# Narrow attention units in the last two batches, masks made on another engine, and a new order of work

## The chip, the cores and the metric

The kernel runs on one core of a Trainium2 chip. A core has TensorE (PE, matrix multiplies; its weight loads are listed as PEld), VectorE (DVE), ScalarE (ACT), GpSimd (POOL) and SyncE (SP). Each of them works through its own queue of instructions in order, and they wait for each other by semaphores. Data comes from the chip's memory by DMA; a DMA is started by an instruction in the queue of POOL or SP. The metric is device time in microseconds (us), lower is better.

## The reference

Two stages, for 8 batches of 576 tokens. The first is attention with 8 heads of 64 dimensions. A query sees itself and the 127 keys before it; a bias that grows linearly with the distance, with a slope for each head, is taken off the scores:

```python
scores = scale * q @ k.T            # scale = 1/8
rel    = pos[:, None] - pos[None, :]
mask   = (rel >= 0) & (rel < 128)
scores = where(mask, scores - slope[h] * abs(rel), -1e9)
attn   = softmax(scores) @ v        # slope[h] = 2 ** -(h + 1)
```

The second takes the heads side by side as x (576 x 512 for each batch) and mixes the tokens:

```python
W   = 1/8 * (x @ w_q) @ (x @ w_k).T     # 576 x 576
out = relu(W @ x) @ w_out
```

The kernel computes W @ x as (x @ w_q) times ((x @ w_k).T @ x), so that the 576 x 576 matrix is never made.

## The kernel before

**Stages of a batch.** For each batch b the kernel makes operations with names that are used below. `L` loads a block of q, k or v, with a conversion from 32 to 16 bit, by a DMA that POOL issues (`Lq`, `Lk`, `Lv` for blocks of 128 tokens, `Lt` for the last 64 tokens of q and k of two batches, and `Lv.4` for those of v). `TQ` and `TT` turn q and k on TensorE, by multiplying with an identity, so that the 64 dimensions of a head lie on the partitions; `ETQ` and `ETT` copy the result from PSUM into `qkT`. The q and k blocks 0 and 1 of batch 0 alone come by SP as 32 bit values and are converted on the chip (`C`).

`QK` computes scores, keys on the partitions and queries along the columns. A unit is 128 keys by 256 queries (the keys' own block and the next) for four of the eight heads; so `add_unit` is called for four groups g of keys and two halves u of the heads, eight units a batch. The last group has 192 + 64 columns, for keys 384 to 511 and the 64 keys after them. A unit fills two PSUM banks with 1024 columns. `EXP` on ACT takes the exponential of these into a tile `pt` (L680), and `MUL` on DVE multiplies with a table of exp(bias), zero where the mask forbids (L687). `PV` uses a piece of `pt` as weights and v with a column of ones as the moving side, so that column 64 of each head is the sum for the softmax; `X` on DVE takes the reciprocal and multiplies (L729, L730), and x is left in 16 bit.

Then `XT` turns x on TensorE, `WQ` and `WK` project it, `G` forms (x @ w_k).T @ x, `MX` multiplies, `RM` applies the relu, `OUT` multiplies with w_out, `EO` copies the result out of PSUM and `DO` sends it off. A name with E in front is the copy out of PSUM, on ACT or DVE.

**Constants.** POOL makes an identity in 32 bit (a memset and an affine select), which DVE converts to 16 bit; it writes the distances with iota, DVE converts them, and POOL sets what the mask forbids to 1e9 with two affine selects. ACT makes the tables `bias` with eight exponentials, one for each head, and DVE copies a second arrangement, `biasl`, for the last group. `zerop` zeroes the end of each `pt`, `ones` sets the column of ones in the v tiles.

**Tiles on TensorE.** Operations differ in how the 128 x 128 array is used, which the kernel calls a mode. Transposes, QK and MX use half the rows (64 x 128, written 64*128 in the profile), so two matmuls on the two halves run together. PV, WQ, WK and OUT use it whole. G uses half the columns (128*64). All matmuls and transposes are issued on L344 and L347.

**The order of work.** The order on each engine is fixed when the program is built. `Order.solve` is a list scheduler: of the operations that can start on an engine within `WINDOW` of the earliest, it takes the one with the lowest number in the table `WANT`, with assumed durations for each operation, four PSUM pairs, and a cost `SWITCH` for a change of mode on TensorE. Results of batches 1 to 5 (`LATE`) are sent from POOL and only after all loads have been issued; the others go by SP. Until 45 us of planned time (`WARM`) gaps on TensorE are filled with multiplies of zeros (`fill`).

Of the kernel before, what the change touches and what calls it, by code (L numbers as in the profile page):

```python
# [14 lines left out]
P = 128  # L15
S = 576
D = 64
# [10 lines left out]
NPT = 5  # L28
PTW = 1088

# [3 lines left out]
STRIDE = 15.2  # L34
BEGIN = {"PE": 0.6, "ACT": 2.0, "DVE": 1.15, "POOL": 1.25, "SP": 0.74, "Q": 0.0}
WARM = 45.0
LAG = 1.1
HELD = 23
# [6 lines left out]
    "ident": -41.18, "idh": 86.52, "iota": -19.88, "dist": -5.89, "zeros": 80.97, "zerop":  # L45
    -1.07, "mask": -22.91, "bias0": -63.72, "bias1": 51.34, "ones0": 9.03, "ones1": -3.39,
    "ones2": 1.11, "ones3": -22.77, "pads": 114.59, "biasl0": 1.04, "biasl1": 135.13, "Cq0.0":
    -16.2, "Ck0.0": -88.36, "Cq0.1": -9.63, "Ck0.1": 2.01, "Lq0.2": -29.16, "Lk0.2": -19.81,
    "Lq0.3": -23.26, "Lk0.3": -32.4, "Lv0.0": -19.56, "Lv0.1": -19.41, "Lt0.0": -19.68, "Lt0.1":
    -19.8, "Lv0.2": -18.96, "Lv0.3": -18.57, "Lv0.4": -18.52, "Lq1.0": -19.26, "Lk1.0": -19.37,  # L50
    "Lq1.1": -19.31, "Lv1.0": 22.81, "Lk1.1": -19.57, "Lw.0": 11.09, "Lw.1": -9.38, "wqq": 9.6,
    "Lq1.2": -17.78, "Lv1.1": 27.97, "Lk1.2": -16.76, "Lq1.3": -17.36, "Lv1.2": 25.83, "Lk1.3":
    -17.32, "Lv1.3": 28.25, "Lwo.0": 22.86, "Lwo.1": 22.17, "Lwo.2": 18.37, "Lwo.3": 22.81,
    "TQ0.0": 34.99, "ETQ0.0": -6.58, "TQ0.1": 52.99, "ETQ0.1": -272.3, "TQ0.2": -141.25,
    "ETQ0.2": -59.41, "TQ0.3": 42.12, "ETQ0.3": 0.07, "QK0.0.0": -12.02, "EXP0.0.0": 42.07,
    "MUL0.0.0": 21.76, "QK0.0.1": 130.94, "EXP0.0.1": -14.28, "MUL0.0.1": -21.15, "PV0.0":
    -15.02, "X0.0": -34.4, "QK0.1.0": -32.06, "EXP0.1.0": -89.58, "MUL0.1.0": -34.39, "QK0.1.1":
    -30.17, "EXP0.1.1": -84.62, "MUL0.1.1": -26.17, "PV0.1": -16.94, "X0.1": -55.8, "XT0.0":
    63.02, "EXT0.0": 6.73, "WQ0.0": -26.32, "EWQ0.0": 45.13, "TT0": -30.36, "ETT0": -52.54,
    "ETT1": -52.67, "QK0.2.0": -30.31, "EXP0.2.0": -89.02, "MUL0.2.0": -34.35, "QK0.2.1": 19.3,  # L60
    "EXP0.2.1": -69.71, "MUL0.2.1": -54.24, "PV0.2": 7.99, "X0.2": -64.32, "QK0.3.0": -21.53,
    "EXP0.3.0": -67.77, "MUL0.3.0": -42.2, "QK0.3.1": 13.11, "EXP0.3.1": -67.85, "MUL0.3.1":
    126.66, "PV0.3": -62.99, "X0.3": -65.12, "PV0.4": -86.99, "X0.4": -63.82, "XT0.1": 75.52,
    "EXT0.1": 12.55, "XT0.2": 53.95, "EXT0.2": -81.4, "WQ0.1": -51.64, "EWQ0.1": 61.61, "WK0":
    18.47, "EWK0": 19.41, "G0": 52.22, "EG0": -68.42, "MX0.0": -35.21, "RM0.0": -24.12, "RM0.2":
    -6.99, "MX0.1": 12.48, "RM0.1": -43.21, "RM0.3": -42.66, "MX0.2": -15.09, "RM0.4": -62.57,
    "OUT0.0": 3.34, "EO0.0": 15.12, "DO0.0": 34.49, "OUT0.1": 15.99, "EO0.1": 48.36, "DO0.1":
    34.7, "OUT0.2": 22.6, "EO0.2": 30.45, "DO0.2": 31.54, "OUT0.3": 22.73, "EO0.3": 55.07,
    "DO0.3": 27.61, "Lq2.0": 25.78, "Lk2.0": 29.91, "Lq2.1": 27.85, "Lv2.0": 36.01, "Lk2.1":
    24.01, "Lq2.2": 30.59, "Lv2.1": 34.45, "Lk2.2": 30.81, "Lq2.3": 31.03, "Lv2.2": 39.03,  # L70
# [117 lines left out]
class Op:  # L188


    def __init__(self, kind, b, part, want, on, deps, emit, banks=0, frees=None, mode=0, half=None):
        self.kind, self.batch, self.part = kind, b, part
        self.name = f"{kind}{b}" + (f".{part}" if part != "" else "")
        self.want, self.on, self.emit = want, on, emit
# [816 lines left out]
```

## Time and profile before

| | |
|---|---|
| median of 3 runs | 140.56 us (140.37 to 140.99) |
| profiled execution | 141.34 us, span 139.5 us |
| granted TensorE clock | 0.997 |
| PE busy | 129.3 us, 93% of the span, 2344 matmuls |
| PEld busy | 81.2 us, 58% |
| ACT busy | 115.2 us, 83% |
| DVE busy | 112.6 us, 81% |
| POOL busy | 110.0 us, 79% |

The span runs from the first to the last instruction of the program. Busy time of PE holds the filler too, 52 matmuls and 15.4 us, and ends of matmuls are modelled, so a busy PE may still be waiting. POOL's busy time is nearly all issue of DMAs.

### The profile page before, as it was taken

Reading aid. Unit: us, or ns where it says so; the run is one execution under the profiler, and the core shown is the slowest. Engines: PE = TensorE matmul, PEld = TensorE weight load, DVE = VectorE, ACT = ScalarE, POOL = GpSimd, SP = SyncE. Lnnn points to the kernel's source line nnn. Section 1 sums busy time; section 2 is a strip of 40 time slices with the busy share of each in tenths; the row PEclk is TensorE's granted clock in tenths of the full one; section 3 lists DMA queues with packets and bytes.
Section 4 is the critical chain, followed back from the end, with each engine's and each line's share of the span. In section 5 each row is a group of like instructions: output and inputs, shape, how many; then the busy total and the mean of one; then the engine's idle time right before and its main releaser. Section 6 shows DMA issues by size and latency. Waiting matters only on the chain.

```text
span 139.5 us, 5462 instructions
## 1 busy us (share of the span) xinstructions
PE 129.3 (93%) x2344; PEld 81.2 (58%) x2344; DVE 112.6 (81%) x250; ACT 115.2 (83%) x175; POOL 110.0 (79%) x145
## 2 busy tenths in 40 slices
PE   6999859998999999988999999999999999999980
PEld 2345447554676367766757567765666666865530
DVE  6648997659987899989999998899999989984400
ACT  6176988399669999999999989999999999676660
POOL 7899988899995899999999999999977745600000
PEclk9999999999999999999999999999999999999998
DMA  4999999999999999999999999999999993730494
GB/s 98 184 180 154 158 153 168 152 146 154 188 215 206 158 159 153 156 155 155 154 156 153 157 156 155 159 153 156 156 215 413 358 327 144 260 153 5 167 320 189
DMA packets 117127, 25.12 MB, mean 180 GB/s; under 512 B 113072, under 2 KB 114096, under 8 KB 117104
## 3 DMA queue, kind: packets, MB, share of 16 engines
q0 software_dynamic: 110912, 20.32, 169.0%
q1 hardware_dynamic: 6192, 4.46, 10.8%
q8 instruction: 18, 0.29, 0.8%
q14 instruction: 5, 0.04, 0.1%
HBM read 29.62 MB, written 9.44 MB: 280 GB/s over the span
## 4 chain that ended last, share of the span: by engine, by line
PE 60%; DVE 16%; POOL 8%; ACT 6%; DMA 5%; issue 2%; ACTq 0%; POOLq 0%; DVEq 0%
PE pair L344 52%; PE pair L347 8%; DVE pt L687 6%; DMA nat<-in_q_dram 5%; POOL nat L506 4%; ACT pt L680 4%; DVE x L730 3%; POOL vt L521 1%; POOL natt L513 1%; DVE inv L729 1%; DVE xtl L730 1%; DVE wqT L353 1%; DVE qkT L359 1%; DVE rm L843 1%; ACT xT L357 1%
## 5 line engine op out<-in xcount | busy, mean ns | idle before, releaser
L680 ACT ACTIVATE pt<-pair 128x1024 f16<-128x1024 f32 x64 | 62.2, 1034 | 2.3 <-PE pair L344 1.7
L687 DVE TENSOR_TENSOR pt<-pt,bias 128x1024 f16<-128x1024 f16 x48 | 32.0, 684 | 2.5 <-ACT pt L680 2.3
L344 PE MATMUL pair<-wout_sb,rm 128*128 128x512 f16 (+1 forms) x132 | 31.7, 373 | 0.2
L521 POOL DMA_DIRECT2D vt<-in_v_dram x32 | 30.1, 995 | 1.6 <-DMA natt<-in_q_dram 0.8
L506 POOL DMA_DIRECT2D nat<-in_k_dram x30 | 29.1, 997 | 0.5 <-DMA nat<-in_k_dram 0.3
L506 POOL DMA_DIRECT2D nat<-in_q_dram x30 | 29.0, 987 | 0.4 <-DMA natt<-in_k_dram 0.4
L344 PEld LDWEIGHTS <-pt 128*128 128x128 f16 x576 | 20.5, 97 | 6.2 <-issue 2.6
L344 PE MATMUL pair<-vt,pt 128*128 128x65 f16 x512 | 22.9, 193 | 0.4 <-ACT pt L680 0.4
L730 DVE TENSOR_TENSOR x<-pair,inv 128x512 f16<-128x512 f32 x32 | 22.1, 692 | 1.1
L344 PE MATMUL pair<-qkT 64*128 64x256 f16 (+2 forms) x320 | 22.1, 250 | 0.6 <-ACT pt L680 0.3
L351 ACT COPY osb<-pair 128x512 f32<-128x512 f32 x29 | 17.0, 596 | 5.7 <-PE pair L344 5.5
L344 PEld LDWEIGHTS <-rm 128*128 128x128 f16 x132 | 11.3, 97 | 11.8 <-issue 1.7
L357 ACT COPY qkT<-pair 128x1024 f32<-128x1024 f32 (+1 forms) x12 | 11.4, 949 | 7.7 <-PE pair L347 7.7
L344 PE MATMUL pair<-fill 128*128 128x512 f16 x52 | 15.4, 430 | 1.8 <-DVE fill L487 1.2
L918 POOL DMA_DIRECT2D out_dram<-osb x20 | 11.2, 574 | 6.6 <-ACT osb L351 3.6
L344 PEld LDWEIGHTS <-qkT 64*128 64x128 f16 x320 | 11.1, 94 | 8.0 <-issue 5.2
L347 PE MATMUL pair<-identh,nat 64*128 64x64 f16 x512 | 10.7, 190 | 1.3 <-DMA nat<-in_q_dram 0.9
L347 PEld LDWEIGHTS <-nat 64*128 64x128 f16 x512 | 9.2, 95 | 4.0 <-DMA nat<-in_q_dram 1.3
L687 DVE TENSOR_TENSOR pt<-pt,biasl 128x1024 f16<-128x1024 f16 x16 | 10.8, 683 | 0.0
L344 PE MATMUL pair<-xT,wqq_sb 128*128 128x320 f16 (+1 forms) x64 | 10.5, 286 | 0.3 <-DVE xT L359 0.3
L357 ACT COPY xT<-pair 128x512 f32<-128x512 f32 (+1 forms) x14 | 7.4, 527 | 3.6 <-PE pair L347 2.9
L359 DVE COPY qkT<-pair 128x512 f16<-128x512 f16 (+2 forms) x14 | 9.3, 686 | 1.3 <-PE pair L347 1.1
(63 smaller groups left out, 165.5 us busy)
## 6 DMA issues: line engine op xcount, KB each, us to landing
out_dram<-osb POOLq DMA_DIRECT2D x20, 256.0 KB, 4.6
vt<-in_v_dram POOLq DMA_DIRECT2D x32, 128.0 KB, 5.9
nat<-in_k_dram POOLq DMA_DIRECT2D x30, 128.0 KB, 6.0
nat<-in_q_dram POOLq DMA_DIRECT2D x30, 128.0 KB, 6.1
out_dram<-osb SPq DMA_DIRECT2D x11, 256.0 KB, 2.3
out_dram<-osb POOLq DMA_DIRECT2D x6, 128.0 KB, 4.2
natf<-in_q_dram SPq DMA_DIRECT2D x2, 256.0 KB, 4.7
natf<-in_k_dram SPq DMA_DIRECT2D x2, 256.0 KB, 5.4
```

The costliest lines, as they stand in the source:

```text
L344: hold(nc.tensor.matmul(*a, **k))
L347: hold(nc.tensor.transpose(*a))
L351: hold(nc.scalar.copy(out_ap, in_ap))
L353: hold(nc.vector.tensor_copy(out=out_ap, in_=in_ap))
L357: hold(nc.scalar.copy(out_ap.bitcast(FP32), in_ap.bitcast(FP32)))
L359: hold(nc.vector.tensor_copy(out=out_ap, in_=in_ap))
L506: return lambda: nc.gpsimd.dma_start(out=nat_s[b % NNAT][j][n], in_=src[b, :, P * n:P * n + P, :].transpose([1, 0, 2]))
L521: return lambda: nc.gpsimd.dma_start(out=vt_s[b % NV][t][:, :, 0:D], in_=v[b, :, P * t:P * t + P, :].transpose([1, 0, 2]))
L680: nc.scalar.activation(out=pt[:, 0:1024], in_=two(s.bank).rearrange("p e c -> p (e c)"), func=AF.Exp, scale=SCALE)
L687: ENG2[o.eng].tensor_tensor(out=pt[:, 0:1024], in0=pt[:, 0:1024], in1=bt, op=ALU.mult)
L730: nc.vector.tensor_tensor(out=x[r].rearrange("p (g h d) -> p g h d", g=2, h=4), in0=pxv[r, :, :, 0:64], in1=inv[r].unsqueeze(3).broadcast_ ...
L918: q.dma_start(out=out[b, P * st:P * st + P, c], in_=osb)
```

## The change

The change has these parts.

- **Narrow units** (`NARROW = (3,)`: the pair of batches 6 and 7). A unit is 64 keys by 192 queries for all eight heads: heads 0 to 3 have their keys on partitions 0 to 63, heads 4 to 7 on 64 to 127. `add_unit` is called as often as before, eight times a batch; unit 7 also holds the last 64 keys. The scores use quarters of the array (64 x 64), a unit has 768 columns, and so have its EXP and MUL. PV (`npv`) multiplies 64 keys at a time, on half of the rows, with two to four blocks of keys for each block of queries. v is loaded in four DMAs a batch, for two heads and all 576 keys each, 64 partitions of 18 rows. A narrow PV waits for all four. The other batches keep the old units (`add_wunit`, `wpv`).
- **Buffers.** `pt` is ten single tiles in place of five pairs. Narrow units use other columns of it, so before the first ten of them an operation `RZ` on DVE zeroes the columns between. The v tiles are used in two layouts, and `ones` is set again when a tile changes layout. QK now lists the release of its `pt` as a need, as EXP did.
- **Constants.** `make_identity` and the affine selects on POOL go. DVE compares the iota with zero for the identity, and makes the mask with multiplies and maxima, once for 256 columns and once for 192. ACT makes a second table of four exponentials for narrow units.
- **The planner.** Each TensorE operation has a count of its instructions. `solve` holds that TensorE's instructions come in blocks of `CHUNK` = 256, that it has `AHEAD` = 191 at first, and that a block comes no sooner than `FETCH` after the one before, and adds the wait.
- **The order.** `WANT` is another table, and `STRIDE`, for defaults, is 13.2 in place of 15.2.

```diff
-NPT = 5
+NPT = 10
 PTW = 1088
+W = 192
+NARROW = (3,)
...
-STRIDE = 15.2
+STRIDE = 13.2
...
+FETCH = 4.8
+CHUNK = 256
+AHEAD = 191
...
+            if eng == "PE" and op.count:
+                gap, wait = at - free["PE"], 0.0
+                if at < WARM and gap > 0.25:
+                    sent += 2 * int(gap / (0.43 if at < COLD else 0.216))
+                while sent > mark:
+                    came = max(at, came + (FETCH if came < 104.0 else FETCH - 1.0) if mark > AHEAD else 0.0)
+                    mark += CHUNK
+                    wait = max(wait, came - at)
+                if sent + op.count > mark:
+                    then = at + wait + occ * (mark - sent) / op.count
+                    least = came + (FETCH if came < 104.0 else FETCH - 1.0) if mark > AHEAD else 0.0
+                    wait += max(0.0, least - then)
+                    came = max(then, least)
+                    mark += CHUNK
+                sent += op.count
+                end, occ = end + wait, occ + wait
...
-    def mk_ident(o):
-        make_identity(nc, ident32)
-
...
-    def mk_mask(o):
-        nc.gpsimd.affine_select(out=wm, in_=wm, compare_op=ALU.is_ge, fill=1.0e9, base=0,
-                                pattern=[[1, 256]], channel_multiplier=-1)
-        nc.gpsimd.affine_select(out=wm, in_=wm, compare_op=ALU.is_ge, fill=1.0e9, base=127,
-                                pattern=[[-1, 256]], channel_multiplier=1)
...
+    def mk_idh(o):
+        nc.vector.tensor_scalar(out=identh, in0=wint[:, 0:P], scalar1=0.0, scalar2=1.0,
+                                op0=ALU.is_equal, op1=ALU.mult)
...
+    def mk_wdist(o):
+        nc.vector.tensor_copy(out=wwm, in_=wint)
+        for s, a in ((-1.0e9, 0.0), (1.0e9, -127.5e9)):
+            nc.vector.tensor_scalar(out=wtmp, in0=wint, scalar1=s, scalar2=a, op0=ALU.mult, op1=ALU.add)
+            nc.vector.tensor_tensor(out=wwm, in0=wwm, in1=wtmp, op=ALU.max)
...
+    def dma_v(b, t, x):
+        return lambda: nc.gpsimd.dma_start(
+            out=vn(b % NV, t)[64 * x:64 * x + 64, :, :, 0:D],
+            in_=v[b, NHP * x + 2 * t:NHP * x + 2 * t + 2, :, :].rearrange("h (n t) d -> t (h n) d", t=64))
...
+    def add_unit(b, g, u):
+        w = base(b, g) + 1.9 * u
+        t = qkT_s[b % 2]
+        s = 2 * g + u
+        pt = pt_s[(8 * b + s) % NPT]
+        ptd = pt[:, 64:PTW].rearrange("p (e a c) -> p e a c", e=2, a=2)[:, :, :, 0:W]
+
+        def em(o):
+            ps = two(o.bank)
+            for a in range(2):
+                for sk, c0, n in ((s, 0, W),) if s < 7 else ((7, 0, P), (8, P, 64)):
+                    for x in range(2):
+                        for e in range(2):
+                            r = slice(64 * e, 64 * e + 64)
+                            mm(ps[64 * x:64 * x + 64, e, W * a + c0:W * a + c0 + n],
+                               t[r, 1, 2 * x + a, 64 * sk:64 * sk + 64],
+                               t[r, 0, 2 * x + a, 64 * sk:64 * sk + n], start=True, stop=True)
...
+            def rz(o):
+                nc.vector.memset(pt[:, 0:1024].rearrange("p (n c) -> p n c", c=256)[:, :, 0:64], 0.0)
...
+        q = add("QK", b, f"{g}.{u}", w, pe(0.175), [*need, *oldp], em, banks=2, mode=3, count=16 if s < 7 else 32)
...
+    def npv(b, qt):
+        sv = [sk for sk in range(2 * qt - 2, 2 * qt + 2) if 0 <= sk < 9]
+
+        def em(o):
+            px = two(o.bank)
+            for a in range(2):
+                for e in range(2):
+                    for i, sk in enumerate(sv):
+                        c = 64 + 256 * (2 * e + a) + 64 * (2 * qt - sk)
...
+                        for x in range(2):
+                            r = slice(64 * x, 64 * x + 64)
+                            h = 2 * a + e
+                            mm(px[:, x, 65 * h:65 * h + 65], pt_s[(8 * b + min(sk, 7)) % NPT][r, c:c + P],
+                               vn(b % NV, a)[r, e, sk, 0:65],
+                               start=(i == 0), stop=(i == len(sv) - 1))
...
-                add_unit(b, g, u)
+                (add_unit if b // 2 in NARROW else add_wunit)(b, g, u)
```

## The prediction

> **What bounds the kernel now.** I read the busy table by stretches first, then the chain that ended last, the groups of matmuls by shape, the POOL rows of the first 8 us, and the DMA queues. Busy time by stretch (columns: us, then busy PE, weight loads, DVE, ACT, POOL with instruction counts, granted clock, DMA share, GB/s):
>
> ```profile
> 0.00:20.00 20.00, 16.67 (x191) 7.93 (x193) 14.62 (x58) 13.56 (x23) 18.58 (x28) 1.00 1.86 155
> 20.00:30.00 10.00, 10.00 (x214) 6.54 (x212) 6.42 (x15) 6.28 (x9) 8.67 (x13) 1.00 1.83 156
> 60.00:95.00 35.00, 33.47 (x742) 23.02 (x740) 32.75 (x64) 33.84 (x51) 35.00 (x42) 1.00 2.42 156
> 95.00:125.00 30.00, 29.23 (x566) 19.38 (x560) 28.17 (x56) 26.83 (x42) 20.06 (x33) 1.00 1.26 249
> 125.00:136.00 11.00, 10.66 (x88) 5.48 (x86) 3.96 (x8) 7.39 (x15) 0.00 (x0) 1.00 0.45 154
> ```
>
> PE, DVE and ACT are nearly full together from 60 to 125 us; after 125 PE alone works off projections. Matmul ends are modelled, so I also added the distances between starts in the trace: what exceeds the streaming time (0.42 ns a column, from 216 ns for 512) by over 45 ns I count as stall. From 20 us to the last matmul that leaves about 101 us of work, 3.2 us of filler and 11.1 us of stall, 2.9 of it between 100 and 130 us. Before 20 us there are only 4.5 us of real work: batch 0 and 1 are loading.
>
> The start of the chain that ended last, from its list in order of time (start, length, what):
>
> ```profile
> 0.56 0.06 issue
> ...
> 1.02 0.29 POOL ident masks.py:199
> 1.31 0.16 issue
> 1.47 1.39 POOL nat L506 x2
> ...
> 6.43 0.06 issue
> 6.49 0.40 POOL wm L430
> ...
> 11.23 1.70 POOL nat L506 x2
> 12.94 6.91 DMA nat<-in_q_dram
> ```
>
> The head is POOL issuing loads, with masks in between, up to the load that TensorE's first transposes of batch 1 (19.9 us) wait for. So the kernel is a head of about 20 us set by loads, then a PE bound of which a tenth is stall.
>
> **The change part by part.** The profiled run took 141.34 us, span 139.5 and 1.84 around it; that is 0.78 above the median of 140.56. I add the terms to 141.34 and subtract 0.78.
>
> 1. Masks leave POOL. What goes, by these rows:
>
> ```profile
> 0.74 0.20 POOL masks.py:197 MEMSET ident<- 128x128 f32 x1 [0.29 <-POOLq L995]
> 1.47 1.05 POOL L506 DMA_DIRECT2D nat<-in_k_dram  x1 [0.16 <-issue]
> 4.28 0.39 POOL L425 IOTA wint<- 128x256 int32 x1
> 6.03 0.40 POOL L428 TENSOR_SCALAR_AFFINE_SELECT wm<-wm 128x256 f32<-128x256 f32 x1 [0.52 <-DVE wm L437]
> 6.49 0.40 POOL L430 TENSOR_SCALAR_AFFINE_SELECT wm<-wm 128x256 f32<-128x256 f32 x1
> 6.84 0.82 POOL L513 DMA_DIRECT2D natt<-in_k_dram  x1
> ```
>
> The first load can start at about 0.77 instead of 1.47 (0.70), and the stretch from 5.51 (end of the fourth load) to 6.84 goes (1.33): POOL's loads come 2.0 us sooner. The iota stays. What is late next is ACT: it runs batch 0's eight exponentials without a break from 12.44 to 19.88, and DVE is 4.93 busy of 5 between 15 and 20. A batch 1 that arrives at 18 meets both. Ends: 0 and -2.0; I take the middle, -1.0.
>
> 2. The masks on VectorE. Five wide operations and seven of 192 columns, nearest row the 128x256 cast at 0.274: about +3.0 us of DVE, and one identity operation for another. DVE is busy 5.8 us of the first 10, so it has room, and the exponential bias, which ran from 6.92 to 9.48 on ACT, is not used before the multiply at 13.50. The second bias table costs ACT four operations of at most 0.40 and DVE two copies of at most 0.58, any time before batch 6. On the path: 0. If the slack were gone, the first casts of q and k (0.57 each, on DVE at 4.48) would slip by one to two operations, +0.5.
>
> 3. PE's work in batches 6 and 7. Scores go from 40 to 72 matmuls a batch, PV from 72 to 136; 192 matmuls more in all, each with its weight load. Wide scores cost 109 ns for two 256-column matmuls that start 3 ns apart, 0.22 a unit, 1.76 a batch. Narrow ones run four at a time on 64x64 quarters: 192 columns are 80 ns, with issue 86; 14 rounds and about 0.2 for the last unit make 1.4. The nearest shape for PV narrow is the transpose of q and k, the same 64x128 weights with 64 columns, 17 ns from start to start: 136 x 17 = 2.31 against 72 x 30 = 2.16 now. Sum -0.2 a batch, -0.4 in all. With the other transposes' pace (21 ns) it is +0.7. I take -0.4.
>
> What carries the rounds of four is the one column-split shape there is:
>
> ```profile
> L344 PEld LDWEIGHTS <-qkT 64*128 64x128 f16 x320 | 11.1, 94 | 8.0 <-issue 5.2 <-ACT qkT L357 1.3 <-ACT rm L841 0.4
> L344 PEld LDWEIGHTS <-wkn 128*64 128x64 f16 x80 | 3.7, 109 | 1.4 <-ACT wkn L351 0.6 <-issue 0.5 <-DVE inv L729 0.2
> ```
>
> A load of 64 columns takes 109 ns, longer than one of 128. At 29.75 us four of them start within 32 ns, which would hide under 80; but in the steady run of that group two start every 109 ns, and there the 256-column matmuls set the pace. If two per 107 ns were the loads' own pace, a round would be 214 instead of 86: 36 rounds, +4.6 us. I take 0, as the four within 32 ns are the same thing that a round needs; 4.6 is the end above. [...]
>
> 4. Exponentials and multiplies. ACT: 1034 ns for 1024 columns and 613 for 512 (the relu) give 0.82 a column, so 768 take 824: 16 x 0.21 = -3.4 us. DVE: 684 for 1024, and 680 against 284 for copies of 1024 and 256, so 768 take 552: 16 x 0.13 = -2.1; added are ten zeroings (RZ) of 128 words, between 0.085 (32 words) and 0.272 (256), say 0.165, +1.7, and two sets of ones, +0.3. So DVE gains nothing. RZ waits for the PV that last read its buffer, and in DVE's queue the evictions X stand behind it, which free PE's banks; placed too early it stalls PE. Of ACT's 3.4 us only what now stalls PE counts: at most the 2.9 us of 100 to 130; at least nothing, or a loss of 0.5 through RZ. I take -0.9.
>
> 5. Loads. Batches 6 and 7 have eight V loads of 1152 rows instead of eight of 1024 and one tail; at POOL's even 0.867 per 1024 that is 7.8 us both ways. A narrow PV waits for all four V loads of its batch instead of one or two; the last load now starts at 99.8 and takes some 6 us, while the first PV of batch 7, the last group of eight, begins at 117.2. Hidden, 0.
>
> 6. Instructions. Added are 384 on PE. The queue list has
>
> ```profile
> q8 instruction: 18, 0.29, 0.8%
> ```
>
> 18 packets of 16 KB for some 4700 instructions: one page per 256. In the trace five intervals lie between the page reads at 94.81 and 125.85 us; 1.5 pages more make 6.5 in the same 31.0 us, 4.8 us each. The closest two now are 4.55 apart, the next closest 5.10 to 5.18, and no matmul but a filler now starts over 0.1 us late without a semaphore to explain it. If 4.55 is possible, nothing is lost; if 5.15 is the least, +2.5. I take a quarter, +0.6. [...]
>
> 7. The order of everything is new. No row shows it; the 11.1 us of stall are what it can win, and its loss has no bound but its like. I take 0, and 2 us either way.
>
> Sum: -1.0 + 0 - 0.4 - 0.9 + 0 + 0.6 + 0 = -1.7. 141.34 - 1.7 = 139.6 in a profile, 138.9 at the median.
>
> **The rivals.**
> - Page reads bind PE in batches 6 and 7 (slower). Place: from the first narrow unit to the last PV, some 95 to 125 us; it decides if reads can't come closer than about 4.8 us. For it: only one interval below 5.1 in the trace. Against: 256 instructions ran in 3.8 us at 36 us with no stall. ACT's gain of 0.9 then goes too: -1.0 - 0.4 + 2.5 = +1.1, 141.7.
> - The column-split loads do not hide: 138.9 + 4.6 + 0.4 for ACT's gain half lost, 143.9. Against: the four within 32 ns.
> - Hidden anyway: ACT's full run to 19.88 eats the earlier loads and PE, not ACT, is what is left after 95 us; terms 1, 4 and 6 are nil, -0.4: 140.2. For it: PE is 29.23 busy of 30 there.
> - The new order also takes 2 us of the 7.7 us of stall between 30 and 100 and the filler of 20 to 30: 136.9. For it: stalls there are single waits of 0.3 to 0.6, not a saturated engine.
> - The new order is worse by 2 to 3 in those same places: 141.4.
>
> **How the numbers follow.** Chances: forecast 0.38 (its own range 138.0 to 139.8), the better order 0.15, hidden 0.15, page reads 0.18, worse order 0.09, column-split loads 0.05. A measurement of this kernel can tell about 0.5% from no change, 139.86 to 141.26. Faster takes the forecast and the better order, and a sliver of hidden: 0.54. Same takes most of hidden and the edges of forecast and worse order: 0.15. Slower the rest, 0.31. The range leaves out the column-split case and the tails of the two orders: 136.6 to 142.3.
>
> **What would show it.** Term 1: first POOL load near 0.8, no affine selects, batch 1's first transposes before 19.9 us. Term 3: quarter matmuls in rounds of four some 86 ns apart, 64x64 weight loads four to a round; PV narrow near 17 ns. Term 4: exponentials of 768 columns near 0.82, multiplies near 0.55, RZ near 0.17. Term 6: page reads closer than 4.8 us, and no stretch of PE idle without a releaser ending about 1 us after a page read. It would be wrong if PE shows such stretches, if 20 us is still where steady work begins, or if stalls after 30 us grow past 11 us.

## The result, and the profile after

The changed kernel takes 142.81 us (median of 4 runs, 142.08 to 143.12), against 140.61 us for the kernel before beside it: a ratio of 1.0147 with a 95% interval of 1.010 to 1.0194. Run again later beside other kernels it gave 1.0109 (1.0066 to 1.0152). It is slower by 1.5 to 2 us; the forecast was 138.9 us. Ratios are of undisturbed executions, and as the profiles of e1 and e7 fell into executions with a lower granted clock (0.976 and 0.982, against 0.994 in the changed kernel's), only their first 20 us are read.

The profiled execution took 142.98 us with a span of 141.0 us, 1.64 and 1.5 us more than before's. Of these 1.5 us, 1.03 lie before the last matmul, which starts at 136.30 in place of 135.28; the rest, 0.4 us, lies behind it, in the last stores. Before's profiled execution was itself 0.78 us above its median, and this one 0.17.

Busy time by stretch of the kernel after (us, then busy PE, weight loads, DVE, ACT, POOL with counts, granted clock, DMA share, GB/s):

```profile
0.00:20.00 20.00, 16.75 (x179) 7.75 (x180) 15.64 (x67) 14.00 (x28) 18.14 (x26) 1.00 1.84 155
20.00:30.00 10.00, 9.50 (x222) 6.40 (x223) 7.97 (x17) 7.99 (x12) 8.71 (x13) 1.00 2.07 163
60.00:95.00 35.00, 34.17 (x713) 22.44 (x710) 33.63 (x74) 33.36 (x46) 34.50 (x41) 1.00 2.42 155
95.00:125.00 30.00, 29.21 (x768) 19.58 (x767) 26.36 (x64) 26.16 (x44) 18.69 (x32) 1.00 1.26 245
125.00:136.00 11.00, 10.84 (x123) 6.11 (x122) 3.41 (x7) 7.48 (x16) 0.00 (x0) 1.00 0.33 116
```

From 95 to 125 us DVE and ACT are relieved by 1.8 and 0.7 us, and PE runs 202 matmuls more at the same busy time; yet PE ends later. The costliest groups by shape (line, engine, operation, out<-in, shape, count | busy us, mean ns | idle before) and the queue of instruction reads on the page:

```profile
L805 ACT ACTIVATE pt<-pair 128x768 f16<-128x768 f32 x16 | 12.6, 830 | 0.1
L813 DVE TENSOR_TENSOR pt<-pt,bias 128x768 f16<-128x768 f16 x14 | 7.6, 549 | 0.7 <-ACT pt L805 0.6
L381 PE MATMUL pair<-vt,pt 64*128 64x65 f16 x272 | 5.8, 190 | 0.7 <-issue 0.7
L798 DVE MEMSET pt<- 128x128 uint32 x10 | 1.6, 165 | 0.1
...
q8 instruction: 20, 0.33, 0.9%
```

The new operations cost what was worked out for them (824, 552 and 165 ns had been assumed). What had not been seen before the change is the third row's ending: 0.7 us of PE idle before a PV matmul, put down to "issue", that is to nothing that the profile shows. In the order of time on PE (start, length, what, idle time before and its releaser):

```profile
41.44 0.61 PE L384 MATMUL pair<-identh,nat 64*128 64x64 f16 x29
42.39 0.23 PE L384 MATMUL pair<-identh,nat 64*128 64x64 f16 x3 [0.34 <-issue]
...
122.31 1.28 PE L381 MATMUL pair<-vt,pt 64*128 64x65 f16 x71
124.25 0.40 PE L381 MATMUL pair<-vt,pt 64*128 64x65 f16 x14 [0.66 <-issue]
```

PE stops in the middle of a run of equal matmuls that wait for no semaphore. The idle times count from modelled ends; from start to start the gaps are 0.53 us (41.86 to 42.39), 0.84 us (123.41 to 124.25) and a third of 0.23 us at 114.37: 1.60 us. Numbered over all matmuls and weight loads that the trace holds, the instructions after the gaps are 1212, 4283 and 4795, which is 188, 187 and 187 above a multiple of 256. (The expectations below count five or six other instructions of PE as well and say 193.) The 16 KB reads of the instruction queue that lie before them ended at 40.95, 113.35 and 122.90, 1.25 to 1.44 us before PE went on. The page of the kernel after has 20 of these reads for its 5074 matmuls and weight loads, that of before 18 for 4688: 254 and 260 for each read. The kernel before has no such gap. I call the place where one block of 256 instructions ends and the next begins a border.

The head changed too. DVE's queue in the kernel after, from the narrow mask on:

```profile
6.14 0.51 DVE L468 CAST wm<-wint 64x192 f32<-64x192 int32 x2
...
8.17 0.45 DVE L473 TENSOR_SCALAR wm<-wm 64x192 f32<-64x192 f32 x1
8.65 0.86 DVE L496 COPY wbiasl<-wbias 128x384 f32<-128x384 f32 x2
9.81 0.81 DVE L547 COPY biasl<-bias 128x256 f32<-128x256 f32 x2 [0.29 <-ACT bias L541]
10.54 0.41 DVE L390 CAST nat<-natf 128x512 f16<-128x512 f32 x1
...
12.17 0.41 DVE L390 CAST nat<-natf 128x512 f16<-128x512 f32 x1
```

The two casts of the second blocks of q and k stand behind the masks and tables and run at 10.54 and 12.17 us; before they ran at 8.23 and 10.26, each as soon as its load had landed. The loads landed at much the same times now (8.56 and 9.97 us, before 8.21 and 10.23). The first exponential starts at 14.27 in place of 12.44 us. This 1.83 us and the 1.60 us of gaps were my two suspects.

### The profile page after: what moved, and what is told of

The parts are those of the page before. It is cut to its first block, busy times and chain, and to the rows that moved or that the text cites. A ratio compares the mean times of both kernels' runs of the same rounds, so it can differ in the third digit from the quotient of the medians.

```text
span 141.0 us, 5860 instructions
## 1 busy us (share of the span) xinstructions
PE 129.5 (92%) x2537; PEld 80.5 (57%) x2537; DVE 113.8 (81%) x279; ACT 115.6 (82%) x177; POOL 108.0 (77%) x140
## 4 chain that ended last, share of the span: by engine, by line
PE 73%; DVE 12%; ACT 8%; issue 4%; DVEq 0%; ACTq 0%
PE pair L381 63%; PE pair L384 10%; ACT pt L764 5%; ACT qkT L394 1%; DVE pt L771 1%; DVE x L884 1%; DVE qkT L396 1%; ACT bias L541 1%; DVE vtl L513 1%; DVE wwm L480 1%; DVE biasl L547 1%; DVE wbiasl L496 0%; DVE xT L396 0%; DVE nat L390 0%; DVE vt L511 0%
## 5 line engine op out<-in xcount | busy, mean ns | idle before, releaser
L764 ACT ACTIVATE pt<-pair 128x1024 f16<-128x1024 f32 x48 | 46.8, 1040 | 3.0 <-PE pair L381 2.9
L381 PEld LDWEIGHTS <-pt 128*128 128x128 f16 (+1 forms) x704 | 20.5, 96 | 8.8 <-issue 4.6
L381 PE MATMUL pair<-vt,pt 128*128 128x65 f16 (+1 forms) x656 | 23.6, 192 | 2.0 <-ACT pt L764 0.8
L771 DVE TENSOR_TENSOR pt<-pt,wbias 128x1024 f16<-128x1024 f16 x36 | 24.1, 682 | 0.5 <-ACT pt L764 0.4
L388 ACT COPY osb<-pair 128x512 f32<-128x512 f32 (+1 forms) x30 | 17.2, 580 | 8.0 <-PE pair L381 8.0
L381 PE MATMUL pair<-qkT 64*128 64x256 f16 (+5 forms) x384 | 21.4, 246 | 1.6 <-ACT pt L764 0.9
L381 PEld LDWEIGHTS <-qkT 64*128 64x128 f16 (+1 forms) x384 | 10.9, 99 | 7.5 <-issue 4.5
L805 ACT ACTIVATE pt<-pair 128x768 f16<-128x768 f32 x16 | 12.6, 830 | 0.1
L997 ACT ACTIVATE rm<-pair 128x512 f16<-128x512 f32 x18 | 10.2, 607 | 0.2 <-PE pair L381 0.2
L381 PE MATMUL pair<-xT,wqq_sb 128*128 128x256 f16 (+1 forms) x64 | 10.3, 287 | 0.0
```

The costliest lines, as they stand in the source:

```text
L381: hold(nc.tensor.matmul(*a, **k))
L388: hold(nc.scalar.copy(out_ap, in_ap))
L764: nc.scalar.activation(out=pt[:, 0:1024], in_=two(s.bank).rearrange("p e c -> p (e c)"), func=AF.Exp, scale=SCALE)
L771: ENG2[o.eng].tensor_tensor(out=pt[:, 0:1024], in0=pt[:, 0:1024], in1=bt, op=ALU.mult)
L805: nc.scalar.activation(out=ptd, in_=two(q.bank)[:, :, 0:2 * W].rearrange("p e (a c) -> p e a c", a=2), func=AF.Exp, scale=SCALE)
L997: hold(nc.scalar.activation(out=out_ap, in_=in_ap, func=AF.Relu, scale=WSCALE))
```

## The experiments

**e1: the narrow tables later.** The seven DVE operations and four exponentials for the narrow mask leave the head; the tables are copied from the wide ones at about 27 us. The order is otherwise kept.

```diff
     def mk_dist(o):
-        for x in range(2):
...
+        pass
...
     def mk_biasl(o):
+        for x in range(2):
+            r = slice(64 * x, 64 * x + 64)
+            nc.vector.tensor_copy(out=nbias[r].rearrange("p e a c -> p (e a) c"),
+                                  in_=wbias[x][r].rearrange("p e a c -> p (e a) c")[:, :, 64 * x:64 * x + W])
...
+    at = next(i for i, op in enumerate(plan) if op.start >= 27.0)
+    plan[at:at] = moved
```

> The changed kernel with its order held fixed, except that the twelve operations for the narrow mask and its exponentials (DVE and ACT) are gone from the head; the two narrow tables are copied from the wide ones on DVE instead, at about 27 us. Theory 1 (constants stand in DVE's queue ahead of the casts of q and k, and the late start is never made up): first exponential back from 14.27 to 12.4 to 12.8 us, and the run 1.3 to 1.9 us shorter, 141.0 to 141.5 where before is 140.6. Theory 2 (block reads of instructions on TensorE are what was lost, 1.5 us in three stalls): the head moves but the end by less than 0.5, 142.3 or more.

Measured: 1.0142 (1.0082 to 1.0201), no gain. The first exponential starts at 14.46 us, not earlier. The two casts on DVE, and PE's queue:

```profile
9.04 0.72 DVE L390 CAST nat<-natf 128x512 f16<-128x512 f32 x1
11.79 0.42 DVE L390 CAST nat<-natf 128x512 f16<-128x512 f32 x1
...
7.41 0.29 PE L384 MATMUL pair<-identh,nat 64*128 64x64 f16 x8 [1.67 <-ACT nat L388]
7.64 2.76 PE L381 MATMUL pair<-fill 128*128 128x512 f16 x12
10.33 0.41 PE L384 MATMUL pair<-identh,nat 64*128 64x64 f16 x16
10.67 2.12 PE L381 MATMUL pair<-fill 128*128 128x512 f16 x9
12.72 0.41 PE L384 MATMUL pair<-identh,nat 64*128 64x64 f16 x16
13.06 1.04 PE L381 MATMUL pair<-fill 128*128 128x512 f16 x4
```

Between the first transposes and the first scores PE has 25 fillers in its queue, 5.9 us, whose number the planner fixed. Both casts ended about half a microsecond before PE turned to them (9.76 and 12.21 us, transposes at 10.33 and 12.72): fillers stood ahead. But this profile tests the masks only in part, for its loads were late: the first k block landed 0.9 us and the second 1.5 us later than in the changed kernel (11.45 in place of 9.97), and the second cast could not run before that. What it shows is that the fillers stand in the way as well; e7 and e11 put both right.

**e2: wide units in the new order.** Batches 6 and 7 compute with units of 128 keys as before, with the old v loads and without RZ, at the places of the new order.

```diff
         def em(o):
             ps = two(o.bank)
+            if b in WIDE:
+                for a in range(2):
+                    hp = 2 * u + a
+                    for kb, q0, wd, c0 in segs(g):
...
         def ml(o):
+            if b in WIDE:
+                wt = (wbias if g < 3 else wbiasl)[u].rearrange("p e a c -> p (e a c)")
+                nc.vector.tensor_tensor(out=pt[:, 0:1024], in0=pt[:, 0:1024], in1=wt, op=ALU.mult)
+                return
```

> The changed kernel with its order held fixed, but batches 6 and 7 compute with the old wide units, old v loads and no RZ in the same places of every queue; the narrow tables are still made and not used. Theory 2: the stalls without a releaser at 114 and 123 us go (1.0 us in all), so the run is 1 us shorter less what ACT's 3.4 us more cost: 141.5 to 143.0. Theory 1: the first exponential stays at 14.27 and the run within 0.5 of the changed kernel's 142.8, as the narrow units are not what was lost. If the narrow units are worth what was forecast (0.9 and 0.4), it is 1.3 longer, 144.1.

Measured: 1.0195 (1.0161 to 1.023), with the last matmul at 136.46, 0.16 us later than with narrow units, and no gap at a border anywhere. With its 1.60 us of gaps taken off, the changed kernel's last matmul would start at 134.70. So narrow units bring about 1.8 us in this order and give 1.6 back at the borders. The loss is there without them too, so the new order is part of it. Neither theory had that: the gaps went as theory 2 said, but the time, 143.18 us, stayed within 0.5 us of the changed kernel, as theory 1 said for another reason.

**e3: only the masks, in the old order.** Identity and mask are made on VectorE and iota comes first on POOL; nothing else differs from before.

```diff
     def mk_ident(o):
-        make_identity(nc, ident32)
+        nc.gpsimd.iota(wint, pattern=[[1, 256]], base=0, channel_multiplier=-1)
...
+        nc.vector.tensor_scalar(out=identh, in0=wint[:, 0:P], scalar1=0.0, scalar2=1.0,
+                                op0=ALU.is_equal, op1=ALU.mult)
...
+        for s, a in ((-1.0e9, 0.0), (1.0e9, -127.5e9)):
+            nc.vector.tensor_scalar(out=wtmp, in0=wint, scalar1=s, scalar2=a, op0=ALU.mult, op1=ALU.add)
+            nc.vector.tensor_tensor(out=wm, in0=wm, in1=wtmp, op=ALU.max)
```

> The kernel before with its order held fixed: iota first on POOL, identity and mask on DVE in the places where the conversions stood, no affine select. The forecast's first term alone: loads from the fifth on 1.5 to 2.0 us sooner, time -1.0, 139.6. Rival (ACT's run of batch 0's exponentials and DVE cover the gain): first exponential still 12.3 to 12.6 us, time within 0.4 of before, 140.2 to 140.9. Theory 1 allows both, as the casts keep their place ahead; it excludes a first exponential after 13.

Measured: 1.0024 (0.9996 to 1.0051), no change. POOL's head in this run:

```profile
0.84 0.33 POOL L422 IOTA wint<- 128x256 int32 x1 [0.39 <-POOLq L996]
1.39 1.04 POOL L507 DMA_DIRECT2D nat<-in_k_dram  x1 [0.21 <-issue]
...
5.03 1.06 POOL L514 DMA_DIRECT2D natt<-in_k_dram  x1
```

The first load starts at 1.39, only 0.08 us sooner than before (1.28 in the changed kernel, where it goes ahead of iota), not at 0.77. The hole of 5.5 to 6.8 us is gone and the fifth load starts 1.81 us sooner (5.03 in place of 6.84), but the first exponential comes only 0.28 us sooner (12.16) and batch 1's first one 0.39 us (22.07). Freeing POOL of the masks is worth nothing measurable.

**e4: masks and narrow units in the old order.** As e3, and batches 6 and 7 with units of 64 keys by 192 queries, whose tables are copied from the wide ones at about 26 us.

```diff
+            if b in NARROW_B:
+                for a in range(2):
+                    for sk, c0, n in ((sn, 0, W),) if sn < 7 else ((7, 0, P), (8, P, 64)):
+                        for x in range(2):
+                            for e in range(2):
+                                r = slice(64 * e, 64 * e + 64)
+                                mm(ps[64 * x:64 * x + 64, e, W * a + c0:W * a + c0 + n],
+                                   t[r, 1, 2 * x + a, 64 * sk:64 * sk + 64],
+                                   t[r, 0, 2 * x + a, 64 * sk:64 * sk + n], start=True, stop=True)
```

> As the run before, and batches 6 and 7 with narrow units in the old order, the narrow tables copied on DVE at about 26 us, RZ just ahead of its exponential; so all of the change but its order. Theory 2: 384 more instructions bring stalls at block boundaries (visible instruction 193 of a block of 256) after 95 us of 0.2 to 0.8 us each, and the run is 0.5 to 1.5 us longer than the one with masks alone. Forecast's terms 3 and 4: 1.3 us shorter than the one with masks alone, no such stall.

Measured: 1.0186 (1.0139 to 1.0232). Beside e3 the last matmul goes from 134.79 to 135.97, by 1.18 us, and nearly all of it is one gap:

```profile
107.96 0.22 PE L358 MATMUL pair<-identh,x 64*128 64x64 f16 x2
109.10 0.42 PE L358 MATMUL pair<-identh,x 64*128 64x64 f16 x14 [0.92 <-issue]
```

From start to start it is 1.13 us, at instruction 4029 (189 above a multiple of 256), 1.64 us after a read ended. So narrow units without the new order run into the same thing. (By the ratios e4 is 2.3 us slower than e3, more than the 0.5 to 1.5 expected; of this the profile shows a span 1.64 us longer.) These two, e3 and e4, left the borders as the suspect to test.

**e5 and e6: the same order, the borders moved.** A few 512-column fillers in the head give way to many of 64 columns, so that all later instructions stand further on in the program.

```diff
-        for _ in range(n):
+        few = FEWER.get(op.name, 0)
+        for _ in range(n - few):
...
+        for i in range(few * (op.name in FEWER) + SMALL.get(op.name, 0)):
+            x = i % 2 if spot.banks == 2 else 0
+            r = slice(64 * x, 64 * x + 64)
+            mm(pairs[spot.bank[0]][:, spot.bank[1] if spot.banks == 1 else x, 0:64], fill[r, 0:P], fill[r, 0:64],
+               start=True, stop=True)
...
+FEWER = {'TQ0.3': 9}
+SMALL = {'TQ0.3': 78}
```

These are the numbers of e5; in e6 they are 3 and 28.

> The changed kernel, same order of work; in the filler run of TensorE ahead of batch 0's second group of transposes, nine fillers of 512 columns (216 ns each) give way to 87 of 64 columns, about the same time, so that every later instruction stands 156 places further on in TensorE's program and the borders of its 256-instruction blocks fall on other work. Theory (a stall comes where a border is reached sooner after the last one than a block read takes: read begins about 2.3 us after the border while loads run and 1.1 to 1.4 us later on, takes 0.95 to 1.5 us, and 1.33 us pass before its instructions go on): the stalls at 41.9, 114.4 and 123.4 us go, and new ones of about 1 us at about 57 us and 1.3 us at about 106 us come, at the new borders; sum 2.4 us in place of 1.6, 143 to 144 us. Rival (the stalls belong to those places in the work, a buffer or an engine that the trace does not name): the same three stalls at the same instructions, 142.8 us.

> As the run before, but three fillers give way to 31 small ones, and the borders move by 56 instructions. Theory of the blocks: by the same sum no border is reached too soon; all three stalls go and none comes, 1.0 to 1.6 us less than the changed kernel: 141.2 to 141.8 us. Rival (the stalls belong to those places in the work): the same three stalls, 142.8 us.

Measured: e5 1.0228 (1.0191 to 1.0264), e6 1.0101 (1.0072 to 1.0129). In e5 the three old gaps are gone, and there are two new ones, 1.14 us at 106.07, where one was expected, and 1.16 us at 44.86, where none was; the one forecast for 57 us did not come. Their sum, 2.29 us where 2.4 was forecast, is luck. The first of them, on PE:

```profile
106.04 0.28 PE L381 MATMUL pair<-qkT 64*64 64x192 f16 x4
107.20 0.28 PE L381 MATMUL pair<-qkT 64*64 64x192 f16 x4 [0.89 <-issue]
```

In e6 one of 1.29 us came at 103.14 although none was expected, and the time lies between its two expectations. All three lie 187 or 188 above a multiple of 256 and end 1.37 to 1.45 us after a read. So the gaps go with the borders and not with the work: the rival falls. Which borders stall, and for how long, I could not forecast.

**e7: the head put right.** Narrow tables late as in e1; DVE casts the second block of q ahead of the tail tables and that of k ahead of both; 8 of the 25 fillers cut to 64 columns.

```diff
+    for name in ("wbiasl0", "wbiasl1"):
+        plan.remove(by[name])
+        plan.insert(plan.index(by["Ck0.1"]) + 1, by[name])
+    plan.remove(by["Cq0.1"])
+    plan.insert(plan.index(by["dist"]) + 1, by["Cq0.1"])
...
+FEWER = {'TQ0.3': 3, 'TQ0.1': 3, 'QK0.0.0': 2}
```

> The changed kernel with its head put right: the narrow tables are copied later from the wide ones (as in the first run), VectorE casts the second half of q ahead of the first tail table and the second half of k ahead of both, and 8 of the 25 fillers of 512 columns between the first transposes and the first scores are cut to 64 columns, so that the count of instructions stays. Theory (the loss of the head is VectorE's queue and TensorE's filler runs together, which is why the first run, that took away the mask operations alone, brought nothing forward): the first exponential starts at 12.3 to 12.8 us in place of 14.27, and 0.9 to 1.6 us of it last to the end: 141.2 to 141.9 us, with the stalls at the block borders still there. Rival (the start is made up for by later slack in any case): the exponential starts earlier but the time stays at 142.4 to 142.9 us.

Measured: 1.0079 (1.0043 to 1.0115), and the first exponential at 12.40 us. The start is repaired as expected. By its ratio the run is 0.4 to 1.0 us faster than the changed kernel (1.0109 and 1.0147), with intervals that overlap; that is near the upper end of what the theory gave (141.9). Whether this comes from the head cannot be read from this profile; e11 bears on it.

**e8: the mask chain in the old head.** As e3, with the seven narrow-mask operations of the change behind the wide ones. Their result is not used.

```diff
+        for x in range(2):
+            r = slice(64 * x, 64 * x + 64)
+            nc.vector.tensor_copy(out=nm[r], in_=wint[r, 64 * x:64 * x + 192])
...
```

> The kernel before with identity and mask on VectorE (141.0 us), and the changed kernel's seven operations for the narrow mask behind them, ahead of the casts of the second halves of q and k; their result is used by nothing. Theory (the 2.5 us of narrow-mask operations stand ahead of the casts and put the first scores off): first exponential at 13.6 to 14.2 us in place of 12.16, the time 0.8 to 1.7 us longer: 141.8 to 142.7 us. Rival (the old order has room for them): first exponential below 12.7 us, 141.0 us.

Measured: 1.0047 (1.0017 to 1.0077), that is 0.3 us beside e3, which the intervals do not part from nothing. The chain does delay the casts, and the first exponential goes from 12.16 to 13.34, but of these 1.18 us only 0.38 are left at batch 1's first exponential:

```profile
13.34 7.44 ACT L691 ACTIVATE pt<-pair 128x1024 f16<-128x1024 f32 x8 [0.51 <-PE pair L345]
22.45 2.19 ACT L691 ACTIVATE pt<-pair 128x1024 f16<-128x1024 f32 x2
```

Before has 22.46 there. A late head is mostly made up for by 22 us; my first theory, that the 1.83 us are half or more of the loss, begins to fall here.

**e9: e4 with its borders moved**, by 42 fillers more of 64 columns (`FEWER, SMALL = {'TQ0.1': 5}, {'TQ0.1': 42}`).

> Masks on VectorE and narrow units in the order of before, as in the fourth run (143.23 us, a stall of 1.13 us at 108 us exactly at a block border); five fillers of 512 columns in the head give way to 47 of 64 columns, so that the borders stand 84 instructions earlier in the work. Reads as they came in the runs so far, laid on this order, give 1.1 us of stalls on the mean in place of 1.9. Theory (the 2 us that narrow units cost in the old order are stalls at borders): 142.2 to 142.6 us, and no stall at 108 us. Rival (they are the narrow units' own work or waits): 143.0 to 143.4 us.

Measured: 1.0114 (1.0071 to 1.0157) against 1.0186, but not for the reason expected: this profile has two gaps, 1.18 us at 95.45 and 1.05 us at 107.14, both 189 above a multiple of 256. (The second one's instruction also has a semaphore to wait for; it went on 1.32 us after a read's end.) With 2.23 us of gaps the last matmul is at 136.50.

**e10: the changed kernel once more.**

> The changed kernel as it stands, once more, beside the runs of this call. All theories: 142.4 to 143.2 us. Theory of the blocks: the order being the same, its stalls stand at the same three places of its program (each at instruction 193 of a block of 256), with other lengths, for the start of a block read differs from run to run; rival (a wait that the trace does not name): the same lengths, 0.5, 0.2 and 0.8 us.

Measured: 142.59 us, 1.0109. The lengths changed and the borders partly too: 0.78 us at 104.36 and 0.23 us at 123.67, none at 41.9 or 114.4. The same program stalls at other borders from execution to execution, always at borders.

**e11: head and borders put right.** e7, with 42 matmuls more in the head (`FEWER = {'TQ0.3': 5, 'TQ0.1': 5, 'QK0.0.0': 2}`, `SMALL = {'TQ0.3': 21, 'TQ0.1': 21}`).

> The changed kernel with its head put right as in the seventh run and the borders moved by 84 instructions (12 fillers give way to 54 small ones). Laid on this order, the block reads of the runs so far give 0.6 us of stalls in place of 1.3. Theory (head and borders are what the change lost): 140.8 to 141.5 us, level with the kernel before. Rival (the new order itself loses as much): 142 us or more.

Measured: 1.0056 (1.0012 to 1.01), about 0.8 us slower than before and the best of the narrow kernels; the time falls between the two expectations. Gaps of 0.54 us (46.98) and 0.43 us (103.02, ending 1.30 us after a read, with a semaphore wait beside it). ACT's exponentials of batch 0, the first of batch 1 and the first of batch 2, in the changed kernel:

```profile
14.27 7.44 ACT L764 ACTIVATE pt<-pair 128x1024 f16<-128x1024 f32 x8 [0.71 <-PE pair L381]
23.54 1.94 ACT L764 ACTIVATE pt<-pair 128x1024 f16<-128x1024 f32 x2 [0.21 <-PE pair L381]
...
39.21 1.02 ACT L764 ACTIVATE pt<-pair 128x1024 f16<-128x1024 f32 x1 [0.22 <-PE pair L381]
```

and in e11:

```profile
12.32 7.45 ACT L765 ACTIVATE pt<-pair 128x1024 f16<-128x1024 f32 x8 [0.49 <-PE pair L381]
22.14 1.94 ACT L765 ACTIVATE pt<-pair 128x1024 f16<-128x1024 f32 x2 [0.76 <-PE pair L381]
...
39.08 1.03 ACT L765 ACTIVATE pt<-pair 128x1024 f16<-128x1024 f32 x1 [0.22 <-PE pair L381]
```

A head that is 1.95 us earlier is 1.40 us earlier at 22 us and 0.13 us at 39 us. So next to nothing of the late head is left by 39 us, and the theory of the head is dropped. (How much of the 0.4 to 1.3 us that e7 and e11 seem to win is the head, and how much shorter gaps, one profile each cannot say.)

**e12: the old kernel with its borders moved.** `FEWER, SMALL = {'TQ0.1': 3}, {'TQ0.1': 28}` in the kernel before, nothing else.

> The kernel before, untouched but for three fillers of 512 columns in the head that give way to 31 of 64 columns, so that the borders of the 256-instruction blocks stand 56 instructions earlier in the work. In the trace of before one stretch then lies between two borders that takes 3.79 us, from 36.0 to 39.8 us; all other blocks after 14 us take 5.1 us or more. Theory (a block goes on no sooner than about 2.4 us until its read begins, 0.95 us for the read and 1.33 us after it: 4.7 us from border to border): a stall of 0.6 to 1.2 us at about 39.8 us, on instruction 193 of a block, with no releaser, in a kernel that had none; no other; the time 0.3 to 1.0 us longer, 141.1 to 141.8 us. Rival (the stalls belong to narrow units or to the new order, not to the borders): no such stall, 140.6 to 141.0 us.

Measured: 0.9994 (0.9961 to 1.0026), no gap at all. The block from 35.46 to 39.25 us took 3.78 us as meant, but its read began at 34.93, 0.5 us ahead of the border and not 2.4 us behind it, and was over 3.3 us before it was needed. So a block of 3.8 us need not stall. In the change the reads of the three blocks that stood still began 3.1, 1.5 and 2.9 us behind the border before (40.01, 111.46 and 122.01 us); what sets that is open. The rival's number came true, but not its reason: e4 stalls in this same old order, and e5 moved the gaps of the same narrow units.

**All runs together.** Start of the last matmul, sum of the gaps at borders (start to start), and the difference, in us:

| kernel | ratio | last matmul | gaps | difference |
|---|---|---|---|---|
| before | 1 | 135.28 | 0 | 135.28 |
| e3, masks, old order | 1.0024 | 134.79 | 0 | 134.79 |
| e8, mask chain | 1.0047 | 135.31 | 0 | 135.31 |
| e12, old, shifted | 0.9994 | 134.69 | 0 | 134.69 |
| after | 1.0147 | 136.30 | 1.60 | 134.70 |
| e10, after again | 1.0109 | 135.96 | 1.02 | 134.94 |
| e5, shifted 156 | 1.0228 | 136.88 | 2.29 | 134.59 |
| e6, shifted 56 | 1.0101 | 136.03 | 1.29 | 134.74 |
| e11, head and borders | 1.0056 | 135.47 | 0.97 | 134.50 |
| e4, narrow, old order | 1.0186 | 135.97 | 1.13 | 134.84 |
| e9, e4 shifted | 1.0114 | 136.50 | 2.23 | 134.27 |
| e2, wide, new order | 1.0195 | 136.46 | 0 | 136.46 |

The seven kernels with narrow units spread from 135.47 to 136.88 with their gaps and from 134.27 to 134.94 without, mean 134.65; the four wide ones in the old order lie from 134.69 to 135.31, mean 135.02. Taking the gaps off assumes that each delays all later work by its full length; that the spread halves speaks for it. Without gaps the change would then be level with the kernel before, or some 0.4 us ahead at the last matmul. The last stores take 0.3 to 0.4 us of that back (span less last matmul: before, e3, e8, e9 and e12 4.3; after 4.7; e2, e5, e6, e10 and e11 4.6 us); as e4, in the old order, has 4.7 as well, this need not be the new order's, and I did not look for its cause.

The gaps can also be counted without looking at borders. Of all matmuls and weight loads after 14 us in these twelve profiles, 11 start more than 0.15 us late, beyond the streaming time of the matmul ahead, with no semaphore event just before them. All 11 lie 187 to 189 above a multiple of 256; with the two that have a semaphore beside them they are the 13 gaps of the table. None of the five kernels with wide units has one.

That narrow units reach their borders sooner can be read from the traces. Of all runs of 256 consecutive PE instructions that begin between 106 and 122 us, the shortest takes 5.18 us before, and the mean 6.8; in the kernel after the mean is 5.0, and 48% take less than 4.8. This does not explain the three early gaps, at 41.9 us (after), 44.9 (e5) and 47.0 (e11): they lie in batches with wide units, in the new order, and e2, e6 and e10 pass there without one.

## Why the prediction was wrong

The profiled executions differ by +1.6 us, the medians by +2.2, and by the ratio of the later run it is +1.5, against a forecast of -1.7. Two steps failed: term 7, which put the new order at 0 where it lost 1.7 us, and term 1, which gave the masks 1.0 us that the runs do not show. A third, term 6, was sized too small: 1.0 to 1.6 us for 0.6. From the last matmul of before to that of after, one profile each, the steps are -0.5 (e3, within the scatter of executions), +1.7 (e2), -1.8 (narrow units) and +1.6 (gaps), in all +1.0; the stores add 0.4. Term by term:

1. *Masks leave POOL*, -1.0: failed. e3 shows 0 (1.0024). The first load moved by 0.08 us there and 0.19 in the change, not 0.70; the later ones did come 1.6 to 1.8 us sooner, for 2.0. The wrong step is what this was worth, the middle between two bounds. It is as the bound of 0 said: the gain is 0.57 us at batch 1's first transposes (19.32 for 19.89) and 0.39 us at its first exponential, and the time does not show it.
2. *Masks on VectorE*, 0 on the path: right in the sum, wrong in the reason. The named cover, that DVE is busy 5.8 us of the first 10, did not hold: the casts of the second blocks slipped by 2.3 and 1.9 us, where 0.5 had been named for the first ones (which run on ACT in the change), since what counted was the place in the queue and not the share. It cost little all the same: in e8 a first exponential 1.18 us later makes at most some 0.3 us of time, and of e11's 1.95 us only 0.13 are left at 39 us.
3. *PE's work*, -0.4: right. Work by start distances falls by 0.55 us (105.40 to 104.85). Narrow PV starts 16 ns apart at the median (17 forecast), the quarter rounds come 82 to 86 ns apart (86) or 101 to 107. The rival of loads that do not hide is out: the 64x64 loads take 106 ns in their row, and no round takes the 214 that it needed. The slower rounds lose some 20 ns to the others; no run shows what makes them so.
4. *Exponentials and multiplies*, -0.9: the durations were right (830, 549 and 165 ns). With term 3 they bring 1.8 us in the new order (e2 to after without gaps; -1.3 forecast), but e3 to e4 and e9 without gaps brings only between 0 and 0.5 us in the old one.
5. *Loads*, 0: right; no row of PE's waits after 100 us names a load.
6. *Instructions*, +0.6: reads of instructions do hold PE up, as the term had it, but the size was off. The gaps are 1.60 and 1.02 us in two profiles of the change, within the 0 to 2.5 given. The quarter was chosen because 4.55 us between reads had been seen. Distances between reads were the wrong row: in the change two reads begin 3.33 us apart (122.01 and 125.34), and PE stood still all the same. What binds is that a block went on 1.25 to 1.64 us after its read's end wherever PE stood still, and the read's beginning varies. The sign named in the forecast, stretches of PE without a releaser that end about 1 us after a read, is what came.
7. *Order*, 0 with 2 either way: this is the other large miss. The new order with wide units (e2) puts the last matmul 1.7 us behind e3. A part of that may be that it was solved for narrow units; the two can't be parted by these runs. Where it falls behind can be read: busy PE in the first 50 us, and of it the fillers (second line of each; its first figure after the length is PE), before:

```profile
0.00:50.00 50.00, 46.09 (x730) 26.11 (x731) 38.60 (x106) 37.35 (x57) 45.01 (x61) 1.00 1.97 165
0.00:50.00 50.00, 15.39 (x52) 4.92 (x52) 0.27 (x1) 1.11 (x4) 1.00 1.97 165
```

after:

```profile
0.00:50.00 50.00, 44.76 (x734) 25.89 (x735) 41.52 (x118) 39.97 (x63) 44.99 (x58) 1.00 2.02 168
0.00:50.00 50.00, 16.40 (x53) 4.96 (x53) 0.27 (x1) 1.11 (x4) 1.00 2.02 168
```

e11:

```profile
0.00:50.00 50.00, 42.90 (x777) 25.45 (x778) 40.95 (x114) 39.47 (x59) 45.12 (x58) 1.00 2.03 169
0.00:50.00 50.00, 14.18 (x95) 4.62 (x95) 0.27 (x1) 1.11 (x4) 1.00 2.03 169
```

e2, which has wide units and no gap:

```profile
0.00:50.00 50.00, 45.23 (x737) 26.11 (x738) 41.85 (x119) 40.63 (x64) 45.13 (x58) 1.00 2.01 167
0.00:50.00 50.00, 16.54 (x53) 4.97 (x53) 0.27 (x1) 1.11 (x4) 1.00 2.01 167
```

Without fillers that is 30.70 us of PE before, 28.36 after, 28.72 in e11, which starts its scores as early as before, and 28.69 in e2. e3, the old order with masks on VectorE too, has 31.20. So the new order has done 2 to 2.5 us less of TensorE's work by 50 us, whatever its head and units. Of e2's 2.5 us, 1.9 arise from 30 to 50 us, 2.0 are still missing at 100 us, and its last matmul is 1.7 us late. What in the order does it I did not look for. The gain of the narrow units is spent on catching this up.

Of the rivals, "page reads bind PE in batches 6 and 7" came nearest in mechanism (141.7 forecast, 142.8 measured): its 2.5 us of reads were 1.0 to 1.6, its -1.0 for the masks was not there, and its condition, that reads cannot come closer than about 4.8 us, did not hold (3.33 us). "The new order is worse by 2 to 3" (141.4) had the other half. The range ended at 142.3. Of what would show it wrong, two signs came as named: stretches of PE idle without a releaser after reads, and a steady state that begins no earlier (batch 1's first transposes at 21.15 us, not before 19.9). The third is undecided: stalls after 30 us, summed by distances between starts, are 10.8 us before, 11.3 in the change and 10.8 in e10.

What stays open: what sets the beginning of a block's read; how much of e2's loss is the order and how much its misfit; and the 0.3 to 0.4 us in the last stores.

## What to carry to other kernels

Count TensorE's instructions beside its time: here smaller tiles left its work nearly alone (105.40 to 104.85 us) and 256 instructions took 5.0 us in place of 6.8 on the mean (106 to 122 us), and the kernels with them lost 0.97 to 2.29 us in gaps. Idle time of PE with "issue" in the midst of equal matmuls at a fixed number modulo 256 (187 to 189 here) is the sign to look for. Before costing a mask or a cast at nothing because its engine is half idle, look at what stands behind it in that queue, and then at how much of a late head is left at the second batch: here (e8) 1.2 us became 0.4. And when a schedule is solved anew, compare busy PE without fillers by stretches; a gain that one part of a change brings can be spent on what the new order lost elsewhere.

## What the runs showed of the hardware

In the twelve profiles of the table a block of PE instructions never went on less than 1.2 us after its 16 KB read had ended, and where PE stood still at a border it went on 1.25 to 1.64 us after. A read took 0.88 to 1.90 us, 0.96 at the median. It began between about 1.2 us ahead of the border before its own and 5.3 us after: about 2.2 us at the median from 60 to 105 us, while loads run, and 1.0 us from 113 to 126 us. A block passed in 3.08 us without a stall in e4 (119.66 to 122.75, read begun 0.76 us after the border) and stalled at 5.15 us in the change (119.12 to 124.27, read begun 2.89 us after). Most borders cost nothing that shows, but single ones up to 1.29 us (e6), and two together 2.3 us in one execution (e5).

The same program stalled at partly different borders in two executions (41.9, 114.4 and 123.4 us; 104.4 and 123.7 us; only the last is the same border), so one profile of such a kernel is a sample.
